# A fused adaLN + segmented attention + squared-ReLU block on one core: the second modulation vector made as columns, the first tiles scaled whole by one engine, and a new order of the work

## The chip, the cores and the metric

The kernel runs on one core of a Trainium2 chip. The metric is the device time of one execution in microseconds (us). Engines are named as in the profile: PE is TensorE (PEld its weight loads), DVE VectorE, ACT ScalarE, POOL GpSimd, SP SyncE, which here issues nearly all DMAs.

## The reference

```python
mod = (silu(c) @ w_mod).reshape(1, 6, 1, -1)          # c: 1x512, w_mod: 512x3072
sa, ca, ga, sb, cb, gb = (mod[:, i] for i in range(6))
h = layernorm(x) * (1 + ca) + sa                       # x: 1x2048x512
x = x + ga * A(h)                                      # 32 heads of 16, 4 segments of 512 rows
h = layernorm(x) * (1 + cb) + sb
x = x + gb * B(h)                                      # relu(h @ w1 + b1)**2 @ w2 + b2, 1792 wide
# A, for each segment s: softmax attention inside the segment with a mask, mixed by a gate with
# a_mem = phi(q) @ M / (phi(q) @ z); then M += phi(k).T @ v, z += sum(phi(k))
```

Everything is float32. The change concerns `sa` and `ca` and the first use of `h`, and the order in which all of the work is issued.

## The kernel before, in words

Rows are in tiles of 128, four tiles to a segment. An f32 operand of a large product is split in two f32r parts, high (an ACT cast) and low (a subtraction on DVE or POOL), and three products of the parts replace one.

The opening, up to the first Q/K product, does this:

- SP loads four tiles of x (`xt`), eight 128x512 pieces of `w_mod` (`wmod`: four for `sa`, slot 0, and four for `ca`, slot 1), and then the three attention weights (`w`, and `X1L` as a buffer for wq).
- DVE and POOL make the statistics and normalize the tiles in place; PE turns each tile with four 128x128 transposes (`blnq`, L613).
- `mod_cols` makes a modulation vector: `mod_parts` multiplies the four pieces of `wmod`, each in its own quarter of the array with silu(c) (`cs`) as the weights, into a bank `bmod` (L570); ACT copies it (`t`, L574); four products with a one-column selector (`selc`, L592) add the quarters and put the vector into columns, `bmodc`; DVE copies those to `modc` (L594).
- `ln_transposed` scales and shifts a turned tile by columns of `modc` (`ln_affine`, `lnf`): for segment 0, ACT does the first two 128x128 pieces (L619) and then DVE the other two (L621). ACT casts the tile into the high part of `HT`, DVE subtracts the low part (both L626). ACT (L704) and POOL or DVE (L708) split the weights in the same way.
- 70 warm-up products `bwarm` of the identity with itself (L542, N_WARM) have no user. They stand in PE's order between the others.

The first Q/K unit (L788 to L790) is 16 steps of three full-height products, eight for Q and eight for K; a step for columns 0 to 255 needs tiles 0 and 1 of `HT`, one for 256 to 511 needs tiles 2 and 3. Later Q/K units (L796) and the value products (L869) run as pairs on the two halves of the array. A unit's banks are copied out by ACT and DVE (`sg`, L830 and L832) and spread by DMAs (`ST`, L848) for the scores (`ba`, L903). Beside the attention, ACT and POOL prepare W1 for the feed-forward part in DRAM (`make_w1`: `X1L`, `w1d`, L738 to L757).

Every piece of work is a node of a plan with an engine, its needs, and buffers that it takes and frees. `ORDER` is a table that gives for each engine the numbers of the nodes in the order in which they are issued; banks and buffers are handed out along it. Each engine works through its own list in order.

Of the kernel before, what the change touches and what calls it, by code (L numbers as in the profile page):

```python
# [17 lines left out]
P = 128  # L18
D = 512
# [38 lines left out]
8-32 3 33-43 94 86 117 96 88 111 44-47 123 48-49 105 50-77 280 290 281-282 291 283-286 292 287 293-297 447-449 333-334  # L58
450 335-336 868 452-454 350 364 455 873 338-340 371 341 379 606-609 385 361 392 611-612 358 613 355 614 316-319 376
367 321 551 322 476 481 323-324 382 732 397 733 400 388 734 404 735 490 407 737 497 738 505 412 878 883 508 739 484  # L60
740 487 416-418 395 420 427 554 522 502 423 430 524 493 435 439 677 635 511 440-441 640 887 556 888 646 563 889 559
890 443 566 892-893 643 571 894 514 895 649 656 530 575 680 576-577 670 579 532 586 1056 589 664 1057 582 1058 652
1059 761 769 803 1061-1062 594 775 598 806 546 599-600 682 996 689 1063-1064 692 920 667 921-922 661 923 548 766 685
925 673 926 772 697 927 782 928 790 778 701-703 705 602 937 712 938 954 939 962 715 940 1131 708 942 968 943 720
944-945 793 1481 724 1191-1192 808 796 1193-1194 787 999 1196-1197 811 799 1198-1199 975 989 725 1002 726 815 959 818
965 823 827 1266 980 831 828-829 834 1326 838 846 1327 971 1328 1089 1329 986 841 1486 1471 1331 983 1332-1333 1134
1097 1334 992 1476 728 1110 850 1137 851 1005 1124 852 1100 1118 1269 1008 1012 854 1015 1094 1024 1103 1020 1028 1025
1115 1035 1272 1026 1031 1106 1121 1038 1224 1235 1043 1047 1232 1238 1140 1048-1049 1143 1490 1147 1127 1491 1155
1150 1492 1229 1493 1051 1245 1159 1253 1163 1160-1161 1404 1166 1495 1170 1496 1259 1173 1497 1241 1498 1178 1401
1359 1182-1184 1275 1256 1540-1541 1282 1250 1542-1543 1278 1186 1285 1545-1546 1290 1364 1547 1262 1548 1380 1373  # L70
1523-1524 1367 1525 1388 1407 1294-1296 1370 1298 1526 1305 1385 1528 1301 1529 1391 1313 1530 1376 1531 1394 1659
1557 1660-1661 1565 1662 1308 1599 1664 1571 1665 1397 1666-1667 1602 1562 1317-1319 1794 1410 1413 1795 1321 1796
1578 1797 1586 2079 1568 1799 1417 1800 1425 1801 1574 1420 1802 1589 1592 2084 1429 1605 1430-1431 1734 1692 2074
1697 1929 1433 1930 1440 1931 1583 1436 1932 1443 1448 1703 2089 1452 1608 1595 1934-1935 1611 1700 1936 1713 1937
1706 1737 1453 1718 1615 1740 1454 1724 1618 1869 1623 1627 1721 1631 1709 1628-1629 1634 1727 1638 1641 1456 1872
1646 1650 1827 1835 1743 1651 1875 1652 1841 1750 2093 1753 1730 2094 1832 1746 2095 1758 2096 1848 1838 1762 1654
1766 1763-1764 1862 1769 2098 1856 1773 2099 1776 2100 1844 2101 1859 1781 2004 1785-1787 2007 1962 2122 1853 1878
2123 1885 2124 1865 1970 2125 1983 1888 2127 1789 1976 2128 1893 2129-2130 2251 1967 2252 1881 2253-2254 1973 2198
1997 538 1897-1899 1991 1901 2256 1908 2257 1979 2258 2156 1994 2259 2139 1904 2140 1988 2141 2161 2142 1911 2167 2144
2000 2145 1916 2170 2146-2147 2177 2191 1920-1922 540 2013 2188 2375 2016 2376 2164 2020 2377 2023 2378 1924 2185 2028  # L80
2380-2381 2173 2382 2301 2306 2383 2322 2182 2032-2034 2036 2499 2043 2500 2046 2309 2501 2194 2502 2315 2280 2504
2039 2505 2312 2506 2051 2285 2055 2201 2507 2288 2204 2056-2057 2291 2208 2318 2211 2059 2216 2220 2224 2227 2221
2231 2294 2010 2222 2234 2446 2239 2641 2243 2404 2297 2244-2245 2418 2651 2644-2647 2409 2325 2328 2654-2655 2661
2415 2332 2335 2656-2657 2340 2412 2247 2425 2344-2346 2348 2355 2439 2664 2671 2665-2667 2351 2421 2674 2681
2675-2677 2363 2528 2542 2684-2685 2721 2686 2536 2430 2358 2724 2687 2725-2727 2691 2436 2533 2449 2367-2369 2433
2456 2464 2694-2695 2731 2696-2697 2442 2459 2452 2371 2734 2701 2735 2774 2736 2549 2563 2539 2737 2468-2470 2472
2545 2479 2704-2705 2560 2475 2482 2706-2707 2487 2573 2554 2766 2741 2770 2762 2491-2493 2557 2576 2580 2744-2746
2583 2566 2570 2495 2588 2747 2711 2592 2596 2603 2593 2599 2606 2611 2714-2717 2751 2594 2615-2617 2754 2619
# [131 lines left out]
2396 2524 2680 2523 2525 2517 2670 2700 2720 2520 2519 2740 2522 2730 2424 2526 2690 2445 2710 2838 2548 2569 2750  # L220
2796-2797 2839 2843 2828 2798 2818 2884 2808 2847 2856 2848 2852 2861 2865 2857 2866 2874 2901 2875 2879 2870 2883
2893 2888 2892 2897 3167-3173 3424-3426 3379 3427-3430 3681-3682 3388 3131 3683 3639 3125 3645 3122 3684 3636 3685
3642 3382 3385 3128 3686-3687 3893 3896 3902 3899
""",
}

# [1394 lines left out]
```

## Time and profile before

| | |
|---|---|
| median of three runs | 764.79 us (761.73 to 765.94) |
| the profiled execution | 762.98 us, its span 761.3 us |
| mean granted TensorE clock | 0.995 |
| busy share PE, DVE, ACT, POOL | 98%, 77%, 58%, 42% |

The opening takes until about 31 us, the attention part until about 440 us, the feed-forward part the rest. In rows of windows the columns are the window, its length, then busy time and instruction count of PE, PEld, DVE, ACT and POOL, the granted PE clock, the DMA share and GB/s. In rows of a timeline they are start, length, engine, line, operation, out<-in, count, and in brackets the idle time ahead and what ended it. In rows of the chain they are start, length and what ran. An f32 product is two records in the trace (one 128x128 product of `bwarm` counts as two), an f32r product or a transpose is one.

### The profile page before, as it was taken

The page shows a single profiled execution, that of the slowest core. Times are in us where ns is not written, and L with a number is a line of the kernel's source. Part 1 is how long each engine was busy: PE and PEld are TensorE (multiplying, and loading weights), DVE is VectorE, ACT ScalarE, POOL GpSimd, SP SyncE. Part 2 cuts the span into 40 slices and gives each one's busy share as a digit, 9 for nine tenths or more (in the row PEclk, how much of TensorE's full clock was granted, in tenths as well). Part 3 has the DMA queues.
Part 4 walks back from the last instruction along what each step waited for, and adds up shares of the span by engine and source line. Part 5 has one row for each costly group of instructions (what it writes and reads, how often), then busy time and mean ns, then how long its engine had stood idle before and what let it go on. Part 6 is the DMA issues. An engine that isn't in the chain of part 4 may idle for free.

```text
span 761.3 us, 18032 instructions
## 1 busy us (share of the span) xinstructions
PE 749.7 (98%) x6649; PEld 598.1 (79%) x6649; DVE 582.7 (77%) x1591; ACT 440.1 (58%) x1001; POOL 322.3 (42%) x400
## 2 busy tenths in 40 slices
PE   9999999999999999999999999999999999999997
PEld 8977676666687667766676679998998899989986
DVE  4587789888899788989989887868855875577544
ACT  2669888899878998678856844636111321221110
POOL 4667777677778777474422542350002002000000
PEclk9999999998999999999999999999999999999999
DMA  9587873554654425355753156753555254448621
GB/s 309 171 239 213 247 206 99 154 148 134 167 161 128 113 80 153 105 141 167 235 170 126 44 194 241 269 200 135 194 194 193 103 208 189 158 161 275 242 92 55
DMA packets 61057, 129.65 MB, mean 170 GB/s; under 512 B 8613, under 2 KB 23977, under 8 KB 59178
## 3 DMA queue, kind: packets, MB, share of 16 engines
q1 hardware_dynamic: 60818, 128.37, 52.8%
q8 instruction: 53, 0.87, 0.5%
q14 instruction: 34, 0.28, 0.1%
q10 hardware_dynamic: 152, 0.13, 0.1%
HBM read 81.29 MB, written 20.19 MB: 133 GB/s over the span
## 4 chain that ended last, share of the span: by engine, by line
PE 86%; ACT 4%; DMA 3%; SPq 2%; POOL 2%; issue 2%; DVE 1%; ACTq 0%; POOLq 0%; DVEq 0%
PE bh L1501 18%; PE bpv L1131 8%; PE bqk L796 7%; PE bpf L1564 7%; PE bpf L1563 7%; PE bpf L1565 7%; PE bpb L1072 5%; PE ba L903 5%; PE bv L869 5%; PE bwop L1233 2%; PE bwarm L542 2%; DMA w1d<-X1L 2%; PE bwop L1235 2%; PE bwop L1234 2%; PE blnq L613 2%
## 5 line engine op out<-in xcount | busy, mean ns | idle before, releaser
L908 DVE CUSTOM_DVE_ANT_0 ba<-ba,msk 128x384 f32<-128x384 f32 (+2 forms) x384 | 192.8, 531 | 34.5 <-PE ba L903 21.3
L1089 ACT ACTIVATE pt<-bpb 128x512 f32<-128x512 f32 x320 | 172.4, 621 | 18.4 <-PE bpb L1072 15.8
L1076 POOL TENSOR_SCALAR_AFFINE_SELECT pt<-pt 128x512 f32<-128x512 f32 x128 | 80.3, 645 | 84.2 <-ACT pt L1089 69.7
L796 PE MATMUL bqk<-HT,WQK 64*128 64x512 f32 x720 | 103.4, 398 | 0.0
L1131 PE MATMUL bpv<-pt,VT 128*32 128x512 f32 (+3 forms) x1024 | 81.5, 441 | 1.4 <-ACT pt L1089 0.9
L1072 PE MATMUL bpb<-ST 64*128 64x256 f32 (+2 forms) x512 | 78.5, 351 | 1.7 <-DVE mx L908 1.2
L796 PEld LDWEIGHTS bqk<-HT,WQK 64*128 64x128 f32 x720 | 68.8, 185 | 10.7 <-DVE mx L908 1.2
L903 PE MATMUL ba<-ST 63*128 63x256 f32 (+2 forms) x512 | 75.1, 346 | 1.5 <-ACT pt L1089 0.7
L1332 POOL TENSOR_TENSOR tt<-h2raw 128x512 f32<-128x512 f32 x8 | 10.9, 1367 | 142.6 <-ACT h2raw L1297 98.6
L1072 PEld LDWEIGHTS bpb<-ST 64*128 64x128 f32 x512 | 51.9, 189 | 21.4 <-ACT pt L1089 4.8
L903 PEld LDWEIGHTS ba<-ST 63*128 63x128 f32 x512 | 48.1, 187 | 24.0 <-ACT pt L1089 5.4
L1527 ACT COPY p<-bh 128x256 f32<-128x256 f32 x28 | 10.4, 371 | 93.1 <-PE bh L1501 64.9
L1501 PEld LDWEIGHTS bh<-ST,w 128*128 128x128 f32 x420 | 56.5, 189 | 3.5
L1501 PE MATMUL bh<-ST,w 128*128 128x256 f32 x420 | 59.0, 282 | 0.0
L1501 PE MATMUL bh<-ST 128*128 128x256 f32 x420 | 58.4, 282 | 0.0
L1501 PEld LDWEIGHTS bh<-ST 128*128 128x128 f32 x420 | 55.8, 190 | 3.1
L908 DVE DVE_READ_ACCUMULATOR2_ANT mx<- 128x1 f32 x384 | 54.2, 141 | 0.0
L1131 PEld LDWEIGHTS bpv<-pt,VT 128*32 128x32 f32 x1024 | 28.2, 109 | 32.8 <-issue 23.0
L1563 PE MATMUL bpf<-w,ST 128*128 128x512 f32 x136 | 53.8, 395 | 0.0
L1545 ACT CAST ST<-xx 128x512 fp32r<-128x512 f32 x43 | 26.1, 619 | 47.6 <-DVE xx L1537 19.1
L1564 PE MATMUL bpf<-w,ST 128*128 128x512 f32 x136 | 53.6, 394 | 0.0
L869 PE MATMUL bv<-WVO,HT 64*128 64x512 f32 x384 | 53.2, 396 | 0.0
(211 smaller groups left out, 1671.1 us busy)
## 6 DMA issues: line engine op xcount, KB each, us to landing
ST<-w1d SPq DMA_DIRECT2D x14, 1792.0 KB
w<-w1d SPq DMA_DIRECT2D x14, 1792.0 KB
ST<-sg SPq DMA_DIRECT2D x192, 128.0 KB
w1d<-X1L SPq DMA_DIRECT2D x21, 512.0 KB
xt<-in_A_x SPq DMA_DIRECT2D x16, 256.0 KB
wm<-in_w_mod SPq DMA_DIRECT2D x16, 256.0 KB
xw<-in_A_x SPq DMA_DIRECT2D x16, 256.0 KB
X1L<-in_B_w SPq DMA_DIRECT2D x7, 512.0 KB
```

The source lines that it names most:

```text
L796: nc.tensor.matmul(bank(banks[w]), W3(w, k, x, cols.start, cols.stop)[r], HT[r, y, k], start=turn == k == i == 0, stop=turn == 1 and k == ...
L869: nc.tensor.matmul(bank(banks[t]), HT[r, x, k, (t2 + t) * P:(t2 + t + 1) * P], WVO[r, k, y], start=turn == k == i == 0, stop=turn == 1 and ...
L903: nc.tensor.matmul(dst[:, c0:c0 + n], ST[b:b + 63, 0, sl, qt * P:(qt + 1) * P], ST[b:b + 63, 1, sl, :n], start=True, stop=True)
L908: nc.vector.tensor_tensor_reduce(i, i, msk[:, 512 - n:], scale=1.0, scalar=-3e38, op0=ALU.add, op1=ALU.max, accum_out=o)
L1072: nc.tensor.matmul(dst, ST[b:b + 64, 1, sl, kb * P:(kb + 1) * P], ST[b:b + 64, 0, sl, q0:512], start=True, stop=True)
L1076: nc.gpsimd.affine_select(out=ap, in_=ap, pattern=[[0, ap.shape[1]], [1, P]], compare_op=ALU.is_ge, fill=0.0, base=0, channel_multiplier=-1)
L1089: ns = [op("ACT", 0.49, lambda j=j: nc.scalar.activation(buf("PPP"[n], pt)[:, i + j], bank(keys[j]), AF.Exp, scale=0.25), pr[slot] + 0.01 ...
L1131: nc.tensor.matmul(bank(o)[32 * hq:32 * hq + 32, q0:q0 + src.shape[1]], v[:, a:a + 32], src, start=start, stop=stop, tile_position=(0, 32 ...
L1501: nc.tensor.matmul(pb(i), A[:, x, kk], B[:, y, kk], start=kk == j == 0, stop=kk == 1 and j == 2)
L1563: nc.tensor.matmul(q, rh, wh, start=(i == 0), stop=False)
L1564: nc.tensor.matmul(q, rh, wl, start=False, stop=False)
L1565: nc.tensor.matmul(q, rl, wh, start=False, stop=(i == NF - 1))
```

## The change

Three things change in the code, and the table of orders is another one throughout.

1. `sa` is made by a new function, `mod_pieces`: for each of the four pieces of `w_mod`, as it lands, four products with a 128x128 block of the piece as the weights and one column of `cs` as the moving operand add into four columns of one bank. The wide product `bmod`, the ACT copy and the selector products are gone for `sa`; `ca` is made as before.
2. In segment 0, tiles 0 and 2 are scaled whole by ACT, tiles 1 and 3 whole by DVE.
3. `ORDER` has new lists for all engines.

```diff
+    def mod_pieces(m, slot, plus, pr):
+        key, b = ("wmod", m), ("modc", m)
+        loads, n = [], None
+        for k in range(KD):
+            loads.append(sp(lambda k=k: nc.sync.dma_start(buf("P", key)[:, k] if not k else TL[key][:, k],
+                                                          wmod[k * P:(k + 1) * P, m * D:(m + 1) * D]),
+                            pr + 0.001 * k, 1 << 18, get=() if k else [("P", key)], soft=loads[:1]))
+
+        def mm(k):
+            for j in range(KD):
+                nc.tensor.matmul(bank(b)[:, j:j + 1], TL[key][:, k, j * P:(j + 1) * P], cs[:, k:k + 1],
+                                 start=k == j == 0, stop=k == j == KD - 1)
+        for k in range(KD):
+            n = pe("F", 1.05, lambda k=k: mm(k), pr + 0.02 + 0.001 * k, after=[n_cs, loads[k], n], get=() if k else [("#D", b)],
+                   put=[key])
+        return dve(4, lambda: nc.vector.tensor_scalar(modc[:, slot, :], bank(b)[:, 0:KD], plus, None, op0=ALU.add),
+                   pr + 0.05, after=[n], put=[b])
...
     def ln_affine(eng, f, q, sc, bi):
-        for k in {"a": (0, 1), "v": (2, 3), "av": range(KD)}[eng]:
+        for k in {"a": (0, 1), "v": (2, 3), "av": range(KD), "vv": range(KD)}[eng]:
             src, dk = q[:, k * P:(k + 1) * P], f[:, k * P:(k + 1) * P]
-            if eng != "v":
+            if eng[0] != "v":
...
-        if low == "POOL":
+        if low == "POOL" or t % 2 == 0:
             af = [op("ACT", 1.38, lambda: ln_affine("av", buf(pool, f), bank(b), sc, bi), pr + 0.01, after=[n, *MODC[sc]], put=[b])]
         else:
-            af = [op("ACT", 0.69, lambda: ln_affine("a", buf(pool, f), bank(b), sc, bi), pr + 0.01, after=[n, *MODC[sc]], put=[b]),
-                  None]
-            af[1] = op("DVE", 0.64, lambda: ln_affine("v", buf(pool, f), bank(b), sc, bi), pr + 0.01, after=[af[0]], put=[b])
+            af = [op("DVE", 1.28, lambda: ln_affine("vv", buf(pool, f), bank(b), sc, bi), pr + 0.01, after=[n, *MODC[sc]], put=[b])]
...
-    n_sa = mod_cols(0, SA, 0.0, PR0 + 0.2, True)
+    n_sa = mod_pieces(0, SA, 0.0, PR0 + 0.2)
...
 ORDER = {
     "PE": """
-8-32 3 33-43 94 86 117 96 88 111 44-47 123 48-49 105 50-77 280 290 281-282 291 283-286 292 287 293-297 447-449 333-334
+8-23 3 24-26 94 27 95-96 28-29 97 30-32 106 86 33 111 121 88 34-41 116 42-56 287 57 288 58-59 289 60-66 290 67-69 291
```

**PE, the opening.** This is PE's list of before from its first instruction to the warm-up products ahead of the first Q/K step (`bcs` is silu(c) turned into columns; a product counts once here):

```order
L542 MATMUL bwarm<-ident 128x128 x25
L532 MATMUL bcs<-ident,crow 128x4
L542 MATMUL bwarm<-ident 128x128 x11
L570 MATMUL bmod<-wmod,cs 32x512 x8
L613 MATMUL blnq<-ident,xt 128x128 x4
L592 MATMUL bmodc<-selc,t 128x1 x8
L613 MATMUL blnq<-ident,xt 128x128 x4
L542 MATMUL bwarm<-ident 128x128 x4
L613 MATMUL blnq<-ident,xt 128x128 x4
L542 MATMUL bwarm<-ident 128x128 x2
L613 MATMUL blnq<-ident,xt 128x128 x4
L542 MATMUL bwarm<-ident 128x128 x28
```

And this is how PE's list begins in the changed kernel (L609 are the one-column products of `mod_pieces`; other lines are those of before, shifted):

```order
L543 MATMUL bwarm<-ident 128x128 x16
L533 MATMUL bcs<-ident,crow 128x4
L543 MATMUL bwarm<-ident 128x128 x3
L609 MATMUL bmodc<-cs,wmod 128x1 x4
L543 MATMUL bwarm<-ident 128x128
L609 MATMUL bmodc<-cs,wmod 128x1 x8
L543 MATMUL bwarm<-ident 128x128 x2
L609 MATMUL bmodc<-cs,wmod 128x1 x4
L543 MATMUL bwarm<-ident 128x128 x3
L632 MATMUL blnq<-ident,xt 128x128 x4
L571 MATMUL bmod<-wmod,cs 32x512 x4
L543 MATMUL bwarm<-ident 128x128
```

Behind these rows it goes on so, into the first steps of the Q/K unit (L805 to L807):

```order
L632 MATMUL blnq<-ident,xt 128x128 x8
L593 MATMUL bmodc<-selc,t 128x1 x4
L543 MATMUL bwarm<-ident 128x128 x8
L632 MATMUL blnq<-ident,xt 128x128 x4
L543 MATMUL bwarm<-ident 128x128 x15
L805 MATMUL bqk<-HT,WQK 128x256
L806 MATMUL bqk<-HT,WQK 128x256
L807 MATMUL bqk<-HT,WQK 128x256
L543 MATMUL bwarm<-ident 128x128
```

Silu(c) comes nine warm-up products earlier, `sa` stands ahead of the first transpose, and of the 70 warm-up products 49 stand ahead of the first Q/K step and 21 between the steps; before, all 70 stood ahead.

**ACT, the opening.** ACT's list of before from the copies of the two modulation products on (`lnf` is the scaling, `HT` the cast of a tile, `WQK` and `WVO` casts of weight columns):

```order
L574 COPY t<-bmod 128x512 x2
L619 ACTIVATE lnf<-blnq,modc 128x128 x6
L704 CAST WQK<-w 128x4x128
L626 CAST HT<-lnf 128x4x128
L704 CAST WQK<-X1L 128x4x128
L619 ACTIVATE lnf<-blnq,modc 128x128 x2
L626 CAST HT<-lnf 128x4x128 x2
L704 CAST WVO<-w 128x4x128
L626 CAST HT<-lnf 128x4x128
```

The same place in the changed kernel:

```order
L575 COPY t<-bmod 128x512
L721 CAST WQK<-X1L 128x4x128
L638 ACTIVATE lnf<-blnq,modc 128x128 x4
L645 CAST HT<-lnf 128x4x128 x2
L721 CAST WQK<-w 128x4x128
L638 ACTIVATE lnf<-blnq,modc 128x128 x4
L721 CAST WVO<-w 128x4x128
L645 CAST HT<-lnf 128x4x128 x2
```

One copy is gone; the eight scalings are two whole tiles, and the first pair of tiles is cast ahead of the second scaling.

**SP, the first loads.** SP's list of before from its start (`xt` are tiles of x, `wmod` pieces of `w_mod`):

```order
L651 DMA xt<-in_A_x 128x512 x3
L555 DMA wmod<-in_w_mod 128x512 x2
L651 DMA xt<-in_A_x 128x512
L555 DMA wmod<-in_w_mod 128x512 x5
L694 DMA w<-in_A_wk 128x4x128
L555 DMA wmod<-in_w_mod 128x512
```

The same in the changed kernel (L603 loads for `sa`, L556 for `ca`):

```order
L668 DMA xt<-in_A_x 128x512 x2
L603 DMA wmod<-in_w_mod 128x512
L668 DMA xt<-in_A_x 128x512
L603 DMA wmod<-in_w_mod 128x512 x2
L556 DMA wmod<-in_w_mod 128x512 x2
L668 DMA xt<-in_A_x 128x512
L603 DMA wmod<-in_w_mod 128x512
L556 DMA wmod<-in_w_mod 128x512 x2
```

The last piece of `sa` is the 10th load and the last of `ca` the 12th, ahead of any weight; the last piece of `ca` was the 13th.

More of the change, by code (lines that the diff above doesn't have):

```diff
@@ L63 @@
[L63 to L67, printed above, removed]
@@ L109 @@
+3862 3855 3860-3861 3859 3790 3866 3864 3870 3793 3791 3794 3792 3812 3863 3865 3796 3795 3874 3867 3869 3814 3811
+3868 3871 3813 3875 3879 3816 3878 3815 3873 3882 3817 3883 3872 3877 3881 3876 3885 3891 3886-3887 3897 3894 3880
+3884 3888
 """,
     "ACT": """
[L111 to L112 removed]
```

295 lines of the change are left out of this document (150 added, 145 removed), and 12 rows, old and new, of the table ORDER.

## The prediction

> **What bounds the kernel now.** I read the head of the page first, then the busy time by stage, then the chain that ended last over the first 33 us, then the timelines of the engines there.
>
> ```profile
> span 761.3 us, 18032 instructions
> PE 749.7 (98%) x6649; PEld 598.1 (79%) x6649; DVE 582.7 (77%) x1591; ACT 440.1 (58%) x1001; POOL 322.3 (42%) x400
> 40.00:220.00 180.00, 175.16 (x2030) 124.39 (x2029) 152.41 (x503) 152.54 (x374) 132.36 (x163) 0.98 0.62 177
> 220.00:440.00 220.00, 219.08 (x2310) 155.21 (x2312) 195.83 (x614) 179.10 (x411) 126.14 (x165) 1.00 0.46 133
> 440.00:760.00 320.00, 317.39 (x2012) 283.90 (x2002) 214.71 (x432) 90.08 (x179) 40.33 (x32) 1.00 0.52 185
> ```
>
> TensorE (PE, the first busy figure of a window) is busy in 98% of the span. In the feed-forward half, 440 to 760 us, the 2.6 us without PE lie in the tail; nothing but less PE work makes that part shorter. The visible slack is in the attention half: 180 − 175.16 = 4.84 us between 40 and 220 us, and a mean clock of 0.98 there. So a step of the opening counts in full if it shifts the moment at which PE has finished its first real products, and what the new order does elsewhere counts where PE waits between 40 and 220 us.
>
> The chain through the opening (start, length, what):
>
> ```profile
> 1.90 7.80 PE bwarm L542 x50
> 9.85 2.65 PE bwarm L542 x22
> 12.50 1.85 PE bmod L570 x16
> 14.94 1.68 PE bmodc L592 x16
> 17.12 0.89 PE bwarm L542 x8
> 18.45 0.45 PE bwarm L542 x4
> 19.33 6.25 PE bwarm L542 x56
> 31.32 2.26 PE bqk L796 x18
> ```
>
> From 1.90 us on PE is never idle: the warm-up products `bwarm` fill every gap, the opening's small products sit between them, and from 19.33 + 6.25 = 25.58 to 31.32 us come the 48 products of the first Q/K unit (16 steps of three, 0.359 us a step). The 70 warm-up products are in both kernels (two records each here, 140 in all). PE takes its queue in order, so a warm-up product is not free filling: it is work ahead of the real one. The first Q/K unit therefore ends at the sum of what stands ahead of it, unless an input is later than that sum. The inputs:
>
> ```profile
> 12.88 0.20 PEld L570 LDWEIGHTS bmod<-wmod,cs 128*32 128x32 f32 x4 [0.30 <-DMA wmod<-in_w_mod]
> 16.66 0.16 DVE L594 TENSOR_SCALAR modc<-bmodc 128x4 f32<-128x4 f32 x1 [0.73 <-PE bmodc L592]
> 16.86 2.43 ACT L619 ACTIVATE lnf<-blnq,modc 128x128 f32<-128x128 f32 x6 [1.77 <-DVE modc L594]
> 18.39 2.00 DVE L621 TENSOR_SCALAR lnf<-blnq,modc 128x128 f32<-128x128 f32 x6 [1.57 <-ACT lnf L619]
> 20.35 1.35 DVE L626 TENSOR_TENSOR HT<-lnf,HT 128x512 fp32r<-128x512 f32 x1
> 22.66 1.93 DVE L626 TENSOR_TENSOR HT<-lnf,HT 128x512 fp32r<-128x512 f32 x3 [0.30 <-ACT HT L626]
> 23.05 0.62 ACT L626 CAST HT<-lnf 128x512 fp32r<-128x512 f32 x1
> 23.57 0.62 ACT L704 CAST WQK<-w 128x512 fp32r<-128x512 f32 x1
> ```
>
> The last of the 13 first loads lands at 12.88 us, the second modulation vector is there at 16.82, the last normalized tile at 22.66 + 1.93 = 24.59. The Q/K products start a microsecond after that, when the warm-up queue is through. The scaling is not the last thing to end; the queue is.
>
> **The change part by part.** *The added vector.* Its way over `bmod`, an ACT copy and `bmodc` goes: half of the 1.85 us and half of the 1.68 us of PE, 0.93 + 0.84 = 1.77 us. In its place stand 16 one-column products, two records each as in `bmodc`, whose operands have the same shape (a 128x128 weight block, one moving column): 32 × 1.68/16 = 3.36 us. Net PE work ahead of the Q/K products: 3.36 − 1.77 = +1.6 us. The per-record price has rows on both sides:
>
> ```profile
> 96.97 0.98 PE bmodc L592 x8
> 128.95 0.84 PE bmr L996 x16
> ```
>
> The same product costs 0.98/8 = 0.122 us later in the kernel (32 × 0.122 = 3.92, net +2.2), and the cheapest small product near it 0.84/16 = 0.0525 (1.68, net −0.1). I take 0.105, the same shape in the same place, and keep −0.1 to +2.2.
>
> Can a piece arrive late? PE's new order has 16 + 3 warm-up products ahead of the first piece. At the rows' rates the 32 records of the 16 end at 9.70 − 18 × 0.12 = 7.5 us (2.65/22 a record; the first ones run slower), the pieces run from about 8.4 to 12.5 us with six warm-ups between them. Their last load is the 10th on SP's queue, that of `bmod` the 12th; the 13th was through at 12.88 us, and PE reaches `bmod` at about 13.8. No wait there. `bmodc` then ends near 16.7 us (16.62 before): ten warm-ups fewer (20 × 0.12 = 2.4) pay for the pieces in front, two transposes more cost 0.9.
>
> *Whole tiles on one engine.* DVE no longer waits 1.57 us for ACT. ACT has two tiles of four 128x128 pieces at 2.43/6 = 0.405 us, DVE two at 2.00/6 = 0.333. From 17.0 us: ACT first tile to 18.7, two casts (0.52 apart, as 23.05 and 23.57) and one of a weight to 20.3, second tile to 21.9, a weight and two casts to 23.5; DVE subtracts the last two (1.93/3 = 0.64 each) by 25.0 us. So the first pair is ready near 21.3, earlier than before, the last tile about where it was. It saves nothing: PE still has 23 warm-ups after `bmodc` (46 records × 6.25/56 = 5.1 us), which puts the first Q/K step at 22.3 us, and 13 more before the step that needs the last pair, at 22.3 + 4 × 0.359 + 26 × 0.112 = 26.6 us. The cover is 1.6 us; if both of DVE's late subtractions took 1.35 us, as one does above, the tile would come at 26.3, still covered. The last of the 70 warm-ups stand between the Q/K steps; added up, the unit ends at 31.32 + 1.6 = 32.9 us.
>
> *Behind it.* Both halves of the unit now end together, where one was copied out at 29.57 before. That costs nothing more if ACT and DVE follow at once:
>
> ```profile
> 29.57 0.59 ACT L830 CAST sg<-bqk 128x512 fp32r<-128x512 f32 x1 [3.30 <-PE bqk L790]
> 33.09 7.86 SPq L848 DMA_DIRECT2D ST<-sg  x12
> 41.55 1.08 ACT L830 CAST sg<-bqk 128x512 fp32r<-128x512 f32 x2
> 44.88 3.29 SPq L848 DMA_DIRECT2D ST<-sg  x4
> 48.90 0.57 SPq L750 DMA_DIRECT2D w1d<-X1L  x1
> 40.00:50.00 10.00, 9.73 (x94) 7.63 (x93) 8.98 (x28) 8.61 (x26) 6.56 (x6) 1.00 0.81 214
> 50.00:62.00 12.00, 12.00 (x109) 9.20 (x107) 10.03 (x35) 6.44 (x23) 7.81 (x9) 1.00 0.80 253
> 62.00:72.00 10.00, 10.00 (x95) 7.70 (x96) 8.05 (x27) 9.89 (x26) 7.36 (x9) 1.00 0.78 224
> ```
>
> SP's fills began 1.8 us after the unit's end and would now begin at 34.8 us, the same shift. The next unit is no longer interleaved with the value products (one group inside it instead of four), so its copy comes near 32.9 + 9 × 2.26/3 + 0.3 = 40.0 instead of 41.55 us, and SP reaches the first write-back of W1 after 20 more issues of 7.86/12, at 34.8 + 13.1 = 47.9 instead of 48.90. That is room for engines that PE did not wait for: from 40 to 72 us PE's idle time is 0.27 us in all. So I give back 0.3 us of the shift there, with an end of 1.6 if later waits absorb all of it.
>
> *The order elsewhere.* Nearly every engine's queue is permuted, by a few places as a rule. Counted in PE's order, changes between full-height, half-height and quarter-width tiles go from 160 to 167. What one costs:
>
> ```profile
> 18.01 0.44 PE blnq L613 x4
> 37.09 0.59 PE blnq L613 x4
> ```
>
> Four transposes between full-height work take 0.44 us, between half-height work 0.59: 0.15 for two changes. Seven more: 7 × 0.075 = +0.5 us (zero, where a wait hides them, to +1.0). The rest of the permutation I cannot price from rows; it is in the rivals.
>
> Sum: +1.6 − 0.3 + 0.5 = +1.8 us. The profiled execution took 762.98 us (761.3 of span, 1.7 around it), which would become 764.8; the median of the three runs shown is 764.79, 1.81 above the profiled one, so on the median's scale 766.6 us. By 0.5%, about what a measurement of this kernel can tell, the line lies at 3.8 us: this forecast is no change. Its own range is 763.1 (pieces at −0.1, the shift absorbed) to 768.0.
>
> **The rivals.** They hang on one place:
>
> ```profile
> 162.00:164.00 2.00, 1.53 (x12) 0.55 (x12) 1.67 (x8) 2.00 (x8) 1.58 (x4) 1.00 0.80 195
> 164.00:166.00 2.00, 1.61 (x54) 1.03 (x52) 0.37 (x2) 1.67 (x5) 1.81 (x5) 1.00 0.78 259
> 166.00:168.00 2.00, 1.73 (x16) 0.77 (x14) 1.97 (x7) 2.00 (x5) 0.83 (x1) 1.00 0.24 74
> 168.00:170.00 2.00, 1.98 (x15) 1.08 (x14) 1.97 (x9) 2.00 (x6) 1.17 (x1) 0.97 0.01 2
> 170.00:172.00 2.00, 2.00 (x22) 1.74 (x23) 1.93 (x10) 2.00 (x7) 1.09 (x3) 0.50 0.00 0
> ...
> 174.00:176.00 2.00, 2.00 (x14) 0.86 (x8) 1.51 (x7) 1.37 (x3) 2.00 (x3) 0.50 0.00 0
> 176.00:178.00 2.00, 2.00 (x26) 1.01 (x24) 1.75 (x8) 1.49 (x4) 0.70 (x2) 0.83 0.18 68
> ```
>
> PE is 1.13 us short over three windows, and then its granted clock is 0.50 for three windows (the one left out reads like its neighbours) and 0.83 for one: 3 × 1.0 + 0.34 + 0.06 = 3.4 us lost.
>
> *Slower: a second such stretch.* If the permuted hand-overs leave three windows in a row near 80% busy at another place between 80 and 220 us, it costs 3.4 us more: 766.6 + 3.4 = 770.0, +0.7%. For it: ACT and DVE are at 85% over these 180 us, so little slack stands behind any hand-over. Against it: it happened once only in 180 us.
>
> *Faster: that stretch goes.* If the new order feeds PE at 162 to 168 us, 3.4 + 1.1 go, and with half of the other 4.84 − 1.13 = 3.7 us of idle time 1.9 more: 766.6 − 6.4 = 760.2, −0.6%. For it: POOL's and ACT's queues are rearranged just there. Against it: places moved are few.
>
> *The pieces bring the stretch into the opening.* Of about 4.1 us, 3.4 are weight loads with one column behind them, almost no array work. If the clock counts that as near idle it falls to half as above: +3.4, 770.0. Against it: 1.68 us of `bmodc` did nothing to the clock.
> The Trainium skill, "TensorE: Matmul & The Clock Gate", section "What's actually happening", says that the clock goes to half after an idle window of about 3.4 us and is otherwise full. By that the pieces, which never leave PE idle, would cost no clock. The trace doesn't agree: PE was never idle that long before 168 us and the clock fell, so I leave this rival a small chance.
>
> **How the numbers follow.** The forecast 0.53; slower by a second stretch 0.24; faster 0.17; the stretch in the opening 0.06. The first lies wholly within 0.5%, the next beyond it above, the third below, the fourth above: faster 0.17, same 0.53, slower 0.30. The range reaches to 760.0, just below the faster rival's price, and to 770.8, above both slower ones; what lies beyond either end is under 0.1 each.
>
> **What would show it.** Right: the one-column pieces at about 0.105 us a record, the first half-height product near 32.9 instead of 31.32 us, no PE wait before it, the last normalized tile near 25 us, and one half-clock stretch as before. Wrong: a PE wait among the pieces or at the last pair; the half-height products starting at 31.3 or earlier; no stretch at 0.50, or two; the feed-forward half, 440 us to the end, shorter or longer by over a microsecond, which no term here allows.

## The result, and the profile after

| | before | after |
|---|---|---|
| median, same chip (7 runs each) | 764.19 us | 770.03 us (768.23 to 772.35) |
| ratio, 95% interval | | 1.0094 (1.0076 to 1.0113) |
| the profiled execution, its span | 762.98, 761.3 | 768.53, 766.8 us |
| mean granted clock of the profiled run | 0.995 | 0.993 |

The change made the kernel slower by 0.94%. (The two medians alone differ by 5.84 us, 0.76%, the lower end of the interval.) The forecast was no change, 766.6 us. The measured time is the price that two of its rivals gave, 770.0, but by luck: each of them adds one half-clock stretch to the forecast, and the sum below is another one.

The head of the page after, and busy time by the prediction's three stages:

```profile
span 766.8 us, 18060 instructions
PE 754.3 (98%) x6665; PEld 602.4 (79%) x6665; DVE 589.4 (77%) x1591; ACT 440.9 (57%) x1000; POOL 320.8 (42%) x400
40.00:220.00 180.00, 175.59 (x2020) 127.88 (x2018) 151.05 (x491) 153.66 (x376) 129.10 (x157) 0.98 0.62 177
220.00:440.00 220.00, 218.31 (x2318) 152.55 (x2315) 196.40 (x620) 177.90 (x409) 128.00 (x170) 1.00 0.47 135
440.00:760.00 320.00, 319.34 (x2024) 284.69 (x2023) 220.04 (x436) 94.32 (x185) 41.28 (x35) 1.00 0.51 182
```

Stages this long hide it: PE is as busy as before and the clock reads 0.98 again. The timeline of one operation that comes at the same point of the work in both kernels, the transposes `bfin` of the attention's output, shows where the time went. Before, then after:

```profile
31.25 2.33 PE L796 MATMUL bqk<-HT,WQK 64*128 64x512 f32 x18
86.73 0.66 PE L1166 MATMUL bfin<-ident,oraw 64*128 64x64 f32 x16
161.28 0.71 PE L1166 MATMUL bfin<-ident,oraw 64*128 64x64 f32 x16
190.22 0.68 PE L1166 MATMUL bfin<-ident,oraw 64*128 64x64 f32 x16
441.86 0.71 PE L1166 MATMUL bfin<-ident,oraw 64*128 64x64 f32 x16
```

```profile
34.84 3.01 PE L813 MATMUL bqk<-HT,WQK 64*128 64x512 f32 x24
94.53 0.65 PE L1183 MATMUL bfin<-ident,oraw 64*128 64x64 f32 x16
169.85 0.71 PE L1183 MATMUL bfin<-ident,oraw 64*128 64x64 f32 x16
193.63 0.67 PE L1183 MATMUL bfin<-ident,oraw 64*128 64x64 f32 x16
446.23 0.71 PE L1183 MATMUL bfin<-ident,oraw 64*128 64x64 f32 x16
```

The first Q/K unit ends 34.84 − 31.25 = 3.6 us late (its end is where the half-height products start; the chain of before put it at 31.32). The shift is 7.8 us at the first `bfin`, 8.6 at 161 us, 3.4 at 190, 4.4 at 442, and 5.6 at the last product (762.57 against 756.99). So +3.6 in the opening, +5.0 between 35 and 161 us, −5.2 up to 190, +1.0 up to 442 and +1.2 in the feed-forward part.

*The opening after.* Windows, then timelines of PE and DVE:

```profile
12.00:14.00 2.00, 2.00 (x16) 2.00 (x15) 1.13 (x4) 0.00 (x0) 0.63 (x1) 0.75 1.02 259
14.00:16.00 2.00, 2.00 (x14) 0.87 (x12) 0.00 (x0) 0.00 (x0) 0.00 (x0) 0.50 1.06 391
16.00:18.00 2.00, 2.00 (x20) 1.33 (x13) 0.00 (x0) 1.11 (x2) 0.00 (x0) 0.90 1.10 349
```

```profile
9.74 1.84 PE L609 MATMUL bmodc<-cs,wmod 128*128 128x1 f32 x16
11.97 0.95 PE L609 MATMUL bmodc<-cs,wmod 128*128 128x1 f32 x8
15.00 1.74 PE L571 MATMUL bmod<-wmod,cs 128*32 128x512 f32 x8
13.58 0.15 DVE L614 TENSOR_SCALAR modc<-bmodc 128x4 f32<-128x4 f32 x1
18.86 0.16 DVE L595 TENSOR_SCALAR modc<-bmodc 128x4 f32<-128x4 f32 x1 [5.12 <-PE bmodc L593]
25.74 2.36 DVE L645 TENSOR_TENSOR HT<-lnf,HT 128x512 fp32r<-128x512 f32 x2
```

Right behind the pieces the granted clock falls to 0.50, with PE busy in 2.00 of 2.00 us all the while. The added vector is in columns at 13.7 us, but the tiles need the other one too, and its row (`bmod`) runs at half clock: columns at 19.02 us, 16.82 before. The last part of a tile ends at 28.10 instead of 24.59.

Two profiles can differ in the opening by themselves. PE's first warm-up products run at about half the later rate (5 to 7 records a microsecond, then 11 or 12), for a time that isn't the same in each execution: `bcs`, which has the same products ahead of it in all kernels that keep before's order there, starts at 9.10 to 10.63 us. Before and after are alike in this (26 records by 6 us in both). Where other openings are compared below, the distance from `bcs` to the unit's end is given too: 21.6 us before, 27.1 after.

*60 to 210 us*, before (first two) and after:

```profile
60.00:110.00 50.00, 49.13 (x637) 35.28 (x635) 41.42 (x147) 45.36 (x109) 38.77 (x44) 1.00 0.75 220
160.00:210.00 50.00, 47.14 (x550) 30.75 (x548) 41.32 (x138) 43.92 (x100) 38.54 (x52) 0.93 0.52 144
```

```profile
60.00:110.00 50.00, 46.10 (x522) 33.41 (x524) 36.75 (x121) 40.49 (x96) 31.77 (x36) 0.93 0.61 175
160.00:210.00 50.00, 49.65 (x620) 33.15 (x620) 44.11 (x146) 48.35 (x114) 41.14 (x58) 1.00 0.53 154
78.00:80.00 2.00, 0.97 (x39) 0.62 (x31) 0.45 (x1) 1.07 (x3) 0.00 (x0) 1.00 0.64 146
80.00:82.00 2.00, 1.33 (x7) 0.87 (x8) 1.93 (x8) 2.00 (x6) 0.85 (x1) 0.82 1.03 378
82.00:84.00 2.00, 2.00 (x43) 1.29 (x45) 1.73 (x10) 1.93 (x5) 2.00 (x3) 0.50 0.08 32
84.00:86.00 2.00, 2.00 (x18) 0.72 (x10) 1.71 (x4) 1.51 (x4) 2.00 (x3) 0.83 0.03 8
```

The two stages have changed places. At 60 to 110 us PE idles 3.0 us more, and there are two stretches at half clock (the one shown, and one at 104 to 110 us), 1.7 us lost in each; at 160 to 210 the idle time and the stretch of before are gone.

ScalarE's waits for W1 at 40 to 110 us, before and after, and SP's write-backs of W1 after (before: 48.90, 54.29 and 59.66 us):

```profile
ACT X1L L747 <- DMA w1d<-X1L: 5.7, 3, 2.7
ACT X1L L764 <- DMA w1d<-X1L: 7.0, 4, 3.0
50.61 1.18 SPq L767 DMA_DIRECT2D w1d<-X1L  x1
58.59 1.28 SPq L767 DMA_DIRECT2D w1d<-X1L  x1
66.81 0.56 SPq L767 DMA_DIRECT2D w1d<-X1L  x1
```

`make_w1` has one buffer for what it writes, so each split on ScalarE waits until the write-back before it has landed; whatever ScalarE has queued behind that split waits too. Before had nearly as much of this wait, but none of its 5.7 us lies between 58 and 88 us; after, 3.5 of the 7.0 lie between 59 and 71 us. There the changed kernel's chain runs over the third write-back, `pt` (ScalarE's exponential of the scores) and PE, but PE's longest wait at 60 to 110 us is another one:

```profile
66.81 3.90 DMA w1d<-X1L
71.34 0.60 ACT pt L1106
71.98 0.50 PE bpb L1089 x2
PE ba L920 <- DVE sg L849: 1.3, 1, 1.3
```

PE stood 0.5 us for `pt` at 72 us, and 1.3 us for DVE's part of a copy `sg` just ahead of the stretch shown, at 80 us.

### The profile page after: what moved, and what is told of

Read it like the earlier page. It is cut to its first block, busy times and chain, and to the rows that moved or that the text cites. A ratio compares the mean times of both kernels' runs of the same rounds, so it can differ in the third digit from the quotient of the medians.

```text
span 766.8 us, 18060 instructions
## 1 busy us (share of the span) xinstructions
PE 754.3 (98%) x6665; PEld 602.4 (79%) x6665; DVE 589.4 (77%) x1591; ACT 440.9 (57%) x1000; POOL 320.8 (42%) x400
## 4 chain that ended last, share of the span: by engine, by line
PE 87%; DMA 4%; POOL 3%; DVE 2%; ACT 2%; issue 2%; SPq 0%; ACTq 0%; POOLq 0%; DVEq 0%
PE bh L1518 17%; PE bqk L813 9%; PE bpv L1148 9%; PE bpf L1580 6%; PE bpf L1581 6%; PE bpf L1582 6%; PE bpb L1089 6%; PE ba L920 6%; PE bv L886 4%; PE bwarm L543 3%; PE bwop L1250 2%; PE bwop L1251 2%; PE bwop L1252 2%; PE blnq L632 2%; DMA w1d<-X1L 2%
## 5 line engine op out<-in xcount | busy, mean ns | idle before, releaser
L925 DVE CUSTOM_DVE_ANT_0 ba<-ba,msk 128x384 f32<-128x384 f32 (+2 forms) x384 | 192.9, 530 | 32.9 <-PE ba L920 21.8
L813 PEld LDWEIGHTS bqk<-HT,WQK 64*128 64x128 f32 x720 | 70.4, 187 | 8.2 <-DVE mx L925 0.3
L1089 PEld LDWEIGHTS bpb<-ST 64*128 64x128 f32 x512 | 49.2, 188 | 24.6 <-ACT pt L1106 5.4
L1580 PE MATMUL bpf<-w,ST 128*128 128x512 f32 x132 | 52.2, 396 | 0.0
L1581 PE MATMUL bpf<-w,ST 128*128 128x512 f32 x132 | 52.0, 394 | 0.0
L1582 PE MATMUL bpf<-w,ST 128*128 128x512 f32 x132 | 51.6, 391 | 0.0
```

The source lines that it names most:

```text
L813: nc.tensor.matmul(bank(banks[w]), W3(w, k, x, cols.start, cols.stop)[r], HT[r, y, k], start=turn == k == i == 0, stop=turn == 1 and k == ...
L925: nc.vector.tensor_tensor_reduce(i, i, msk[:, 512 - n:], scale=1.0, scalar=-3e38, op0=ALU.add, op1=ALU.max, accum_out=o)
L1089: nc.tensor.matmul(dst, ST[b:b + 64, 1, sl, kb * P:(kb + 1) * P], ST[b:b + 64, 0, sl, q0:512], start=True, stop=True)
L1580: nc.tensor.matmul(q, rh, wh, start=(i == 0), stop=False)
L1581: nc.tensor.matmul(q, rh, wl, start=False, stop=False)
L1582: nc.tensor.matmul(q, rl, wh, start=False, stop=(i == NF - 1))
```

## The experiments

Ratios are to before on the same chip, with 95% intervals; 1 us is 0.0013.

**The two halves of the change.** A plan can take one kernel's order up to a step and the other's behind it.

```diff
 old opening, new rest: code of before
 ORDER: before's up to the first Q/K unit and its copies, the changed kernel's behind
```

> Before's code and before's order of the opening (through the first Q/K unit and its copies), and the changed kernel's order for everything behind it. Theory A, the whole loss is the opening's 3.5 us carried to the end: this runs like before, 763.5 to 765, and the first Q/K unit ends at 31.3 us. Theory B, the opening costs 3.5 us and the new order of the rest costs about 2 of its own (4.5 lost at 60 to 105 us, 4.5 won at 160 to 205, 2 lost behind): 765.5 to 767, with 8 us lost at no place but about 4.5 us by 110 us. Theory C, the loss at 60 to 105 us comes from the late opening and not from the order there: without it only the gain at 160 to 205 is left, 760 to 762.

Measured: 769.19 us, 1.0079 (1.0052 to 1.0107). In its profile the unit ends at 31.35 us, PE is busy 46.45 of 50 us at 60 to 110 with two half-clock stretches, 80 to 84 and 104 to 108. Theory A falls, theory C for this part too: the order behind the opening loses by itself. Theory B had the kind of the loss, but with 765.5 to 767 us not its size.

```diff
 new opening, old rest: the changed code
 ORDER: the changed kernel's up to the first Q/K unit and its copies, before's behind
```

> The changed kernel's code and order of the opening, and before's order for everything behind it. Theory A and theory B both: 764.2 + 3.5 = 767 to 768.5, with the first Q/K unit's end at 34.8 us; under B the shift against before stays at about 3.5 us from 35 us to the end, with before's stretch at half clock at 168 to 176 us now at 171 to 180. Theory C, the late opening itself brings the loss at 60 to 105 us: the shift grows to 8 us by 110 us and stays, 771 to 773.

Measured: 768.68 us, 1.0081 (1.0060 to 1.0103). The shift is 3.7 us at the unit's end and 5.0 at 442 us and at the end, with a new half-clock stretch at 84 to 90 us beside the old one, now at 176 to 182. Each half alone loses nearly what both lose together, so the losses don't add.

**The parts of the opening, alone.**

```diff
 pieces alone: before's code and order
-    n_sa = mod_cols(0, SA, 0.0, PR0 + 0.2, True)
+    n_sa = mod_pieces(0, SA, 0.0, PR0 + 0.2)
```

> Before's code and order with the added vector in four pieces alone: the four pieces stand where the four products of its row stood, and the row's copy and its turn go. If the pieces themselves bring the half clock (32 records with one moving column each, 1.6 us net of PE work and 1.9 us of clock): first Q/K unit ends at 34 to 35 us, granted clock 0.50 for about 3 us right behind the pieces, 767 to 768.5 in all. If the half clock comes from the new order of the opening (pieces early, before the second product of the warm-up is through): the clock stays at 1.00, the unit ends at 32.5 to 33, 765 to 766.5. If PE's work in the opening lies beside something else: 764 to 765.

Measured: 770.17 us, 1.0090 (1.0068 to 1.0112). The pieces, and the clock in windows behind them:

```profile
12.75 3.63 PE L608 MATMUL bmodc<-cs,wmod 128*128 128x1 f32 x32
18.00:20.00 2.00, 2.00 (x12) 1.88 (x10) 0.00 (x0) 0.21 (x1) 0.00 (x0) 0.50 1.06 373
20.00:22.00 2.00, 2.00 (x11) 2.00 (x12) 0.20 (x2) 1.57 (x4) 0.00 (x0) 0.50 1.06 378
22.00:24.00 2.00, 2.00 (x11) 2.00 (x11) 1.33 (x4) 0.32 (x1) 0.00 (x0) 0.51 1.05 385
```

The unit ends at 36.67 us, 5.4 late (5.0 from `bcs`), where 34 to 35 was expected: the half clock held from 17 to 24 us, not for 3 us. 4.5 us are left at 442 us and at the end. Nothing behind the opening takes much back. The pieces alone cost what the whole change costs.

```diff
 whole tiles alone: before's code and order
-        if low == "POOL":
+        if low == "POOL" or t % 2 == 0:
```

> Before's code and order with the scaling of segment 0's tiles by one engine alone: two tiles of each four whole on ScalarE, two whole on VectorE. All theories: no change that can be measured, 763.5 to 765, first Q/K unit's end within 0.5 us of 31.3. If the later tiles (2.36 us on ScalarE in the changed kernel for a whole one) hold up the Q/K steps: the unit ends 1 us or more later and the time is over 765.

Measured: 763.69 us, 1.0000 (0.9985 to 1.0015): nothing. In its profile all of the opening is 1 us late, `bcs`, columns and unit alike; from the last columns to the unit's end it is 14.4 us, as before.

**Is it the few moving columns?**

```diff
 wide pieces alone: the run with the pieces alone, and
-                nc.tensor.matmul(bank(b)[:, j:j + 1], TL[key][:, k, j * P:(j + 1) * P], cs[:, k:k + 1],
+                nc.tensor.matmul(bank(b)[:, 64 * j:64 * j + 64], TL[key][:, k, j * P:(j + 1) * P],
+                                 cs[:, k:k + 1].to_broadcast([P, 64]),
 (and the same in the changed kernel: wide pieces)
```

> The run with the pieces alone, and one edit: each piece's products move 64 equal columns (the condition's column repeated) where they moved one; the copy that adds the vector reads every 64th column. The pieces alone ended the first Q/K unit 5.4 us late, with the granted clock at 0.50 from 17 to 24 us. If few moving columns bring the half clock: the clock stays at 1.00 through the opening, the unit ends about 2 us late (33.3 us), 764.5 to 766 in all. If the half clock comes from something else at that place (the weight loads, four products at a time to quarters of the array, the transposes): it stays at 0.50 for about 6 us, 768 to 770.5.

Measured: 767.29 us, 1.0055 (1.0033 to 1.0077).

```profile
18.00:20.00 2.00, 2.00 (x20) 2.00 (x21) 0.16 (x1) 1.44 (x4) 0.00 (x0) 1.00 1.04 364
```

The clock stays at 1.00, and the unit ends at 32.96 us: +1.71, or +2.2 from `bcs`, which starts 0.53 us earlier here (about 1.9 of PE's net work, and 0.2 in which PE waits for the copy of CA's row). The time is 1.3 us above the range that was expected; its profile is 1.7 us behind at the unit's end, 2.9 at 442 us and 3.7 at the end. The mean granted clock of its twelve timed runs is 0.9947, that of before beside them 0.9969. By that 0.0022 × 765 = 1.7 us of the loss would be the clock (an estimate); where it fell in them is not shown.

> The changed kernel with the same edit: pieces of 64 moving columns. If few moving columns bring the half clock: 1.00 at 13 to 16 us, the first Q/K unit ends at about 33 us and not at 34.84, and the time falls by 1.5 to 2 us to 768 to 768.5. If not: 0.50 stays at 13 to 16 us, 769.5 to 770.5.

Measured: 767.52 us, 1.0045 (1.0026 to 1.0063). The clock is 1.00, the columns are there at 17.10 us, the unit ends at 32.92: 1.92 earlier than in the changed kernel, and the columns 1.92 earlier too. `bcs` starts 0.30 us earlier here; from it to the unit's end it is 25.5 us and not 27.1, so 1.6 us are the clock's. In this profile, the slowest of the ten timed runs, none of that is left at 442 us (`bfin` at 446.41); the median is 2.5 us below the changed kernel's, on another chip.

```diff
 fewer warm-up products: the changed kernel without eight that nothing reads
-        pe("F", 0.22, lambda: nc.tensor.matmul(bank(wk_)[:, :P], ident, ident, ...), ...
+        pe("F", 0.22, (lambda: None) if 26 <= i < 34 else (lambda: nc.tensor.matmul(...)), ...
```

> The changed kernel without eight of the 70 warm-up products (those between the columns of CA and the third tile's turn, 0.38 us each, 3.0 us of PE work that computes nothing). If PE's queue alone sets the end of the opening: the first Q/K unit ends at about 31.8 us, 767 in all. If the scaled tiles set it (the last pair of tiles was there at 28.1 us, and its step began at 28.6): the unit ends at 34.3 or later, PE stands idle before it, and the granted clock may fall there; 769.5 to 772.

Measured: 769.97 us, 1.0082 (1.0055 to 1.0109). The unit ends at 34.78 us, 0.4 us earlier from `bcs`. Eight products are 2.0 us and not 3.0 (16 records take 2.03), but most of it doesn't show: PE now waits in the first Q/K step.

```profile
23.28 0.38 PE L806 MATMUL bqk<-HT,WQK 128*128 128x256 f32 x1 [0.17 <-DVE HT L645]
24.41 0.38 PE L807 MATMUL bqk<-HT,WQK 128*128 128x256 f32 x1 [0.75 <-POOL WQK L725]
```

So in the changed kernel the tiles and the weight's split come within 0.4 us of setting the unit's end, and the queue of warm-up products, in which PE never waits there, just covers them.

**Where the new order loses.** Before's code, and a later switch each.

```diff
 ORDER: before's up to PE's step 270 (123 us), 186 (81 us) or 146 (62 us), the changed kernel's behind
```

> Before's code, and before's order up to about 123 us (the first 270 steps of PE and all that they need), the changed kernel's order behind it. If the gain of the new order at 160 to 205 us stands by itself: 4 to 4.5 us less than before, 758 to 760, with no stretch at half clock at 168 to 178 us. If it was only the loss at 60 to 105 us given back (work that had been moved back there): no gain, 762 to 764.

Measured: 763.32 us, 0.9994 (0.9975 to 1.0014), no half clock at 160 to 210 us in its profile. The gain is not there: in its profile `bfin` is 4.2 us late where before's reads 171 us, 2.3 early at 190, 1.4 early at 442 and the end 0.6 late.

> Before's code, and before's order up to about 62 us (the first 146 steps of PE and what they need), the changed kernel's order behind it. The switch at 31 us lost 6 us against before, the switch at 123 us none. If the loss at 60 to 105 us is made by the order of 31 to 62 us (the write-backs of the scaled W1 and the loads that come later in SP's queue): none of it is left, 762 to 765, PE busy over 49 of 50 us at 60 to 110. If it is made by the order behind 62 us: PE busy 46.5 of 50, two stretches at half clock at 80 to 108 us, 767 to 770.

Measured: 767.08 us, 1.0053 (1.0033 to 1.0072).

```profile
70.83 0.62 ACT L747 CAST X1L<-X1L 128x512 fp32r<-128x512 f32 x1 [3.73 <-DMA w1d<-X1L]
70.00:72.00 2.00, 0.00 (x0) 0.00 (x1) 0.00 (x0) 1.17 (x3) 0.00 (x0) 0.90 0.86 197
```

> The same with the switch at about 81 us (the first 186 steps of PE). If the loss is made before 62 us: like the switch at 62, 762 to 765. If between 62 and 81 us: none of it left here, and the switch at 62 shows it. If behind 81 us: both show it, 767 to 770.

Measured: 762.80 us, 0.9994 (0.9977 to 1.0011). The loss of the switch at 62 us is made by the order of 62 to 81 us, and there ScalarE waits for a write-back of W1, with `pt` behind it, for which PE waits (2.40 us in the run that switches at 62).

**Which wait it is.**

```diff
 three W1 steps forward: the changed kernel
 SP:   second write-back two places earlier, third one four places earlier
 POOL: low half of the third split four places earlier
```

> The changed kernel with three steps of the first W1 tile moved forward and nothing else: its second write-back ahead of two copies of sg in SP's queue (59.97 us's place to about 55.5), the low half of its third split ahead of the sums of phi on GpSimd (64.44 to about 61), and the third write-back ahead of five copies in SP's queue (66.81 to about 62). The switches at 62 and 81 us put the loss between them, where ScalarE stands 2.65 and 0.83 us at a split of X1L that waits for a write-back of W1. If that wait is the cause: it falls under 1 us in all, PE is busy over 48 of 50 us at 60 to 110 (46.1 now), and 2 to 4.5 us go: 765.5 to 768. If it is another difference of the order there: PE's 46 of 50 stay, 769 to 771.

Measured: 768.29 us, 1.0071 (1.0047 to 1.0096); PE is busy 47.87 of 50 us at 60 to 110. Inconclusive: of the two waits aimed at, the one of 0.83 us went and the one of 2.65 stayed (2.68), and at 45 to 65 us ScalarE waited no less than in the changed kernel (5.6 there):

```profile
ACT X1L L764 <- DMA w1d<-X1L: 6.1, 2, 3.4
14.00:16.00 2.00, 2.00 (x18) 0.99 (x18) 0.00 (x0) 0.00 (x1) 0.00 (x0) 1.00 1.05 396
```

In this profile the clock stayed at 1.00 in the opening, with the changed kernel's own pieces and its own order there, and from `bcs` to the unit's end it took 25.5 us, as with 64 columns. So the fall is not certain in every execution, and 1.6 us is its price again.

```diff
 one write-back later: before; SP's list, 174 is the third write-back of the first W1 tile
-... 370 475 174 630 528 629 634 626 631 628 627 632 ...
+... 370 475 630 528 629 634 626 631 628 627 174 632 ...
```

> Before's kernel with the same step moved the other way: its third write-back of the first W1 tile stands in SP's queue behind eight copies and loads more (issued at about 66.3 us and not at 59.66). If this one place makes the loss: ScalarE waits about 3.5 us at the next split, PE 2 to 3 us, half clock for 4 to 8 us behind it, 766.5 to 768.5. If the loss needs more than that: 763 to 765.

Measured: 766.81 us, 1.0047 (1.0030 to 1.0064). One step, moved eight places in a list of DMA issues, shows on ScalarE (which had no wait at this split before), on PE and, in this profile, in the clock:

```profile
68.95 0.62 ACT L747 CAST X1L<-X1L 128x512 fp32r<-128x512 f32 x1 [3.08 <-DMA w1d<-X1L]
70.12 1.45 PE L613 MATMUL blnq<-ident,xt 128*128 128x128 f32 x8 [1.44 <-ACT pt L1089]
72.00:74.00 2.00, 2.00 (x14) 1.61 (x12) 1.41 (x4) 2.00 (x8) 1.81 (x3) 0.50 0.82 216
```

Over the timed runs the mean granted clock is no lower than that of before beside them (0.998 and 0.997). So these 3.4 us are PE's waits and not, on the whole, the clock.

```diff
 one write-back earlier: the run that switches at 62 us
-... 475 519 518 520 629 623 632 624 528 625 174 633 ...
+... 475 174 519 518 520 629 623 632 624 528 625 633 ...
```

> The run that switches the order at 62 us, with one step moved: the third write-back of the first W1 tile stands in SP's queue nine loads and copies earlier, where before has it (issued at 59.66 us there, at 66.78 in the run that switches at 62). In that run ScalarE stood 3.73 us at the next split of X1L until this write-back had landed, PE 2.40 us behind it, and the clock went to 0.50 at 72 to 78 us. If this one place in SP's queue makes the loss: no wait of ScalarE over 1 us there, no half clock at 70 to 80, 762.5 to 764.5 like before. If something else of the order of 62 to 81 us does: 766 to 768.

Measured: 766.90 us, 1.0045 (1.0021 to 1.0068). The wait for the write-back is gone and the clock stays at 1.00 there, yet the time is hardly less. Another load now ends the wait:

```profile
66.27 0.62 ACT L747 CAST X1L<-X1L 128x512 fp32r<-128x512 f32 x1
77.34 1.09 ACT L1089 ACTIVATE pt<-bpb 128x512 f32<-128x512 f32 x2 [2.27 <-DMA wm<-in_w_mod]
```

So a late write-back is enough to lose 3.4 us in before's order, but it is not the only thing that the new order has late in SP's queue at 62 to 81 us (`wm` are pieces of `w_mod` for a later vector).

**A version that beats both.** Loads of the tiles first, CA's row ahead of most pieces, fewer warm-up products.

```diff
 CA first: wide pieces alone, and
 PE: ... first piece, CA's row, second piece, CA's columns, third and fourth piece, turns ...
 SP: four tiles, wmod 0 first quarter, wmod 1, wmod 0 the rest; 24 warm-up products left out
 128 columns: pieces of 128 moving columns, two turns ahead of the last pieces, 18 left out
 128 columns, switch at 81: that opening, the changed kernel's order from 81 us
```

> Before's code and order with pieces of 64 moving columns, placed so that they don't delay CA's columns: the tiles' loads first, then one quarter of wmod 0, the four of wmod 1, the other three of wmod 0; on PE the first piece, CA's row, the second piece, CA's columns, the last two pieces; 24 of the 70 warm-up products left out, which stood ahead of the Q/K steps. Theory, the opening's end is set by the columns of the modulation and the chain of tiles behind them (14.5 us from the end of the last copy of columns to the end of the first Q/K unit before, and again 14.5 in the run with wide pieces alone): the last copy of columns ends at 14.9 to 15.5 us and not at 16.8, the unit at 29.5 to 30, 1.3 to 1.8 us less in all than before. Rival, something else ends at 31 us by itself (a weight's split, the loads): the unit stays at 31 to 31.5 and the time is before's. Rival, fewer warm-up products bring the half clock: 0.50 behind 20 us, 764 to 767.

Measured: 762.17 us, 0.9981 (0.9961 to 1.0001). The last columns were there at 15.37 us, but the clock fell at 15 to 19 us in spite of 64 columns, the turns (the tiles' transposes) came late, and the unit ended at 30.83, where 29.5 to 30 was expected.

> The run with CA first once more, with pieces of 128 moving columns (as many as a warm-up product has) and two of the tiles' turns ahead of the last two pieces; 18 warm-up products left out and not 24. In that run the clock stood at 0.50 at 15 to 19 us all the same, and the turns came late (ScalarE waited 3.9 us for the first). If few moving columns are what brings the half clock and 64 were still too few: 1.00 through the opening, the first Q/K unit ends at 29.5 to 30.2 us, 761 to 762. If not: 0.50 again at about 15 to 19 us, the unit ends at 30.5 to 31, 762 to 763.

Measured: 761.71 us, 0.9979 (0.9961 to 0.9998). Clock 1.00 through the opening; but the last columns came at 16.90 (the last two pieces stood behind two turns, and the first piece waited 0.6 us for its load), the unit ends at 30.85, again later than expected.

> The same opening, and the changed kernel's order from about 81 us on (the switch at 81 us ran at before's time in the median, 2.5 us less in its profile). If the two add up: 1.3 to 1.8 us for the opening and 0 to 2.5 for the order, 759.5 to 761.5, the fastest of all. If the order's gain is lost again: like the run beside it, 761 to 763.

Measured: 761.45 us, 0.9972 (0.9957 to 0.9987), faster than both kernels.

```diff
 old feed-forward order: that run, with before's order of the feed-forward steps in their places
```

> The run with pieces of 128 columns and the switch at 81 us, with before's order of the feed-forward part's steps in the places where they stand. In the eight profiled runs that have the new order there, the shift against before grew by 0.8 to 2.0 us between 442 us and the end; in those with before's order there it stayed within 0.1 (but for one, +0.3). If the new order of that part costs this: the shift stays level from 442 us on and the time is 1 to 1.5 us less than that of the run beside it. If the growth comes from what is upstream: it stays, and the two take the same time.

> The run with pieces of 128 columns and the switch at 81 us once more, as the neighbour of the one above on the same chip: 0.9957 to 0.9987 of before again, 760.5 to 762.5, with the shift against before growing by about 1 us in the feed-forward part.

Measured: 760.63 us, 0.9970 (0.9954 to 0.9986), beside 761.11, 0.9976 (0.9959 to 0.9994): the 1 to 1.5 us that were expected between them are not there, and the two times can't be told apart. The expectation's count of the profiles was too neat. From the last `bfin` to the last product it is 315.1 to 315.9 us in the nine profiles with before's order of that part (mean 315.3; this run 315.4), 315.7 to 317.1 in the eleven with the new one (mean 316.4). The new order costs about 1.1 us there by the profiles.

## Why the prediction was wrong

*Right:* the work of the pieces. 32 records in 3.63 us where they stand together (pieces alone) are 0.113 each, 0.105 was taken; the net cost was put at 1.6 us and is 3.63 − 1.77 = 1.9. The unit's end was put at 32.9, and with the clock held up (64 columns) it is 32.92; that close it is by luck, since that opening started 0.3 us early. Whole tiles cost nothing that could be measured. No piece came late in the changed kernel.

*Wrong, step by step.*

1. "The pieces bring the stretch into the opening" had 0.06. It happened, and it is the step that failed first: the clock took 1.6 us more of the opening, which with 1.9 of work makes about the 3.6 us by which the unit was late (1.6 was forecast). My reason against it, that 1.68 us of `bmodc` did nothing to the clock, leaned on a run of such products less than half as long. In the profiles the clock fell in the opening in four of five with one-column pieces, one of three with 64 columns, none of four with 128 and none of eight without pieces. That is one execution of each; the mean granted clock over the timed runs agrees: 0.990 for pieces alone and 0.995 with 64 columns, 0.992 for the changed kernel and 0.996 with 64, 0.997 before. Whether it is the columns that keep the clock up at 128 is less sure: those runs have another order of the opening too. The Trainium skill, "TensorE: Matmul & The Clock Gate", section "What's actually happening", sets the fall behind an idle window of about 3.4 us and calls that window free-running. The first doesn't agree with 2.00 of 2.00 us busy; the second would let the same opening keep its clock once in a while, as the run with three W1 steps forward did, but no run here shows the window itself.

2. "The scaling is not the last thing to end; the queue is" no longer holds after the change: with 2.0 us less of the queue the unit ended 0.4 us earlier. The pieces delay CA's row, and that delays the tiles. DVE's last two subtractions, put at 0.64 us each, took 1.18 us each: even with the clock up (64 columns) the last tile came at 26.18 us, not near 25.0. The vector that was made faster was not the one that came last.

3. "That is room for engines that PE did not wait for" failed: 0.3 us were to come back behind the opening, and 5.0 more were lost by 161 us. The first write-back of W1 was put at 47.9 us and came at 50.61, the third at 66.81 instead of 59.66. PE's small idle time at 40 to 72 us showed that nothing was late there before; it didn't show how far SP's, ScalarE's and PE's queues were from it.

4. "The rest of the permutation I cannot price" left the main term out of the sum. One step of it is worth 0.47% in before's order. And the rivals were treated as cases of which one comes: here two new stretches came, the old one went, and the opening had its own, all in one kernel. In the switches at 81 and 123 us the old stretch went from the profile and the mean granted clock rose (0.998 and 0.999, 0.997 before), and still no time was won: 0.9994 both times.

5. The feed-forward part was allowed a microsecond and took 1.2; its own order accounts for it in the profiles, not in the timed pair.

The term of +0.5 for tile shapes stays untested, and so does what else the new order has late at 62 to 81 us beside the write-back and the load of `wm`. How much of the changed kernel's own loss is the write-backs' stays open too: the one run that moved them there left the larger wait in place, and the longest wait of the changed kernel's PE at 60 to 110 us was for `sg`. Why the two halves' losses don't add was not settled; in the run with the new opening and before's order, ScalarE waited 2.76 and 1.77 us for the same write-backs.

## What to carry to other kernels

Where both inputs of a step are needed, look which one comes last before making the other faster. A product with one moving column keeps PE busy in the profile and can still cost the clock; if such products must stand in a row, give them as many columns as a filler product has (128 here), and let them replace fillers. Price a new order by the steps that an in-order engine waits for with work of others behind it: here a write-back with a single buffer.

## What the runs showed of the hardware

The granted clock went to 0.50 with PE busy in every window, within a microsecond behind 3.6 us of one-column f32 products that stood together (pieces alone), and behind the same products with six records of fillers among them (the changed kernel, pieces from 8.62 to 12.9 us, 0.50 from 13 us); in one of five profiles with one-column pieces it did not fall. Such a product of 128 moving columns costs 1.95/16 = 0.122 us a record (the runs with 128 columns) and one of a single column 0.113 (3.63/32, pieces alone), so the columns are almost free there. DVE's last two subtractions of the opening took 1.18 us each, with POOL subtracting for a weight from 26.2 to 27.6 us beside them; before, three took 0.64 each from 22.66 us, with POOL idle for nearly all of that time, and the one at 20.35 us, with POOL subtracting beside it, took 1.35.
